# Seven quarter products per group in the first multiplication, the nonlinearity split, and one sum by transfer

## The chip, the cores and the metric

One core of one Trainium2 chip runs the whole computation in one launch. The metric is the device time of the program in microseconds (us), and lower is better. The core's engines work side by side, each through a queue of its own in program order: TensorE (PE, with its weight loads as PEld), VectorE (DVE), ScalarE (ACT), GpSimd (POOL), and SyncE (SP), which issues transfers.

## The reference

Attention with a causal window of 64, for 8 batches, 8 heads, 576 positions and 64 channels, is followed by a feed-forward layer with a PReLU between its two products. All arrays are fp32.

```python
scores = (q @ k.T) / sqrt(64);  mask = (0 <= rel) & (rel < 64)
attn = softmax(where(mask, scores, -1e9));  a = attn @ v
x = a.transpose(0, 2, 1, 3).reshape(4608, 512)
h = x @ w_in                              # 512 x 2048
g = maximum(h, 0) + alpha * minimum(h, 0) # alpha: one value for each of the 2048 columns
out = g @ w_out                           # 2048 x 512
```

The kernel returns `out`, 4608 x 512.

## The kernel before

The 4608 tokens are 36 tiles of 128, and four tiles make a block (9 blocks, `BT` = 4). Every fp32 product is made of three products of split numbers: a value is the sum of a high part (`xh`, `wh`) and a low part (`xl`, `wl`), and hi*hi, hi*lo and lo*hi are accumulated.

**First stage.** For each block, 16 cells (`cell`, L621), one for each 128 of the 2048 columns of `w_in`: 12 matmuls of 512 tokens (3 splits by 4 slices of the 512 channels, L637) into one of two PSUM banks. ACT reads the bank and writes slope*h to an SBUF cell (L643), DVE makes the PReLU from the bank and the cell (L644), and SP stores the cell to DRAM (`hidden`, L648). Attention runs between the cells. Twice in a block there is a turn (`attend_two`, L592): scores of two tiles (L444), then the values of the two tiles before (L500). Between the two, DVE takes the row minimum (L453), ACT the exponential (L460), POOL scales (L469), and the weights are turned by 16 small DVE transposes for each tile (L477, L479), or for the tiles in `PE_TURNED` and the first eight by PE (L484) with a copy out of PSUM (L488). `x_parts` (L561) splits the result into the block's x.

`w_in` and `w_out` come as raw 64-bit words and are converted on the chip (`chunk`, L332). `convert_out` (L376) forms the seven combinations of `w_out`'s quarters that the second stage needs, for one of four groups d (`DUOS`) at a time, in blocks 1, 3, 5 and 7. Slots 0 to 11 of `w_hi` and `w_lo` keep twelve of the 28 forms; the other 16 go to DRAM in two parts, and come back into `w_in`'s slots 12 to 27 at the end of the first stage (`fetch_weights`, L666).

**Second stage.** For each block and d (36 units, `second`, L691), the four quarters of g (a11, a12, a21, a22) are fetched (L701, issued up to 45 us of planned time ahead). DVE makes four sums z1 to z4 (L708). Seven forms are split into y parts by ACT (L713) and DVE (L714), and seven products of 12 matmuls with 256 columns (L741) accumulate over d in seven PSUM banks. These are the seven products of Strassen's scheme in Winograd's form, in place of eight. After four units, ACT (L758) and DVE (L749) add the banks up to the block of `out`.

**Order.** Each operation is registered with `Program.add`, with its durations, reads and writes. `Program.order` (L84) simulates the engines and writes out every engine's queue in that order: on each engine the ready operation with the earliest due time goes next. PE's due times are the keys (`begin_of`, `CELL`, `UNIT`, `STEP`); those of the others follow from what waits for them. While no real product is ready at the start, PE gets dummy matmuls (`warm`, L304), until the first cell.

## Time and profile before

| | |
|---|---|
| median of 3 runs | 844.79 us (844.37 to 847.77) |
| the profiled execution | 848.35 us |
| its span, first to last instruction | 846.6 us |
| PE busy | 838.7 us (99%) |
| DVE busy | 690.4 us (82%) |
| ACT busy | 446.5 us (53%) |
| POOL busy | 201.0 us (24%) |

The span is 1.75 us shorter than the execution's own time, and that execution took 3.56 us more than the median. Busy time is the union of an engine's instructions. PE's instructions overlap in the pipeline, so the distance between two starts says what one costs, and its duration does not. The profile's rows that are used are in a section of their own below.

### The profile page before, as it was taken

How to read it: one execution, taken by the hardware profiler on the slowest of the kernel's cores; microseconds unless marked ns; L12 is line 12 of the kernel's file. 1: busy time of each engine (PE TensorE's matmuls, PEld its weight loads, DVE VectorE, ACT ScalarE, POOL GpSimd, SP SyncE). 2: the span in 40 equal slices, each digit the busy share in tenths (PEclk: the TensorE clock that was granted, in tenths of full speed). 3: DMA queues.
4: the chain of work that ended last, by engine and by line, in shares of the span. 5: the costliest groups of instructions: out<-in, count | busy, mean ns of one | idle time of the engine just before them, and what ended most of it. 6: DMA issues, size and time to landing. Idle time of an engine off the chain costs nothing.

```text
span 846.6 us, 21125 instructions
## 1 busy us (share of the span) xinstructions
PE 838.7 (99%) x7856; PEld 760.3 (90%) x7856; DVE 690.4 (82%) x1775; ACT 446.5 (53%) x1130; POOL 201.0 (24%) x188
## 2 busy tenths in 40 slices
PE   9899999999999999999999999999999999999998
PEld 8788888888888888888888889999999999999998
DVE  5777898997989989899884547979888888979883
ACT  6789765556554664546644334444444444444441
POOL 5788492106511164212640000000000000000000
PEclk9899999999999999999999999999999999999999
DMA  7787755555655667556556997535444443535211
GB/s 235 235 275 240 232 173 165 168 177 190 205 174 163 209 219 252 192 176 216 196 204 184 316 330 231 165 110 168 121 148 138 136 151 125 154 110 169 83 37 50
DMA packets 121287, 152.91 MB, mean 181 GB/s; under 512 B 10592, under 2 KB 92512, under 8 KB 121184
## 3 DMA queue, kind: packets, MB, share of 16 engines
q1 hardware_dynamic: 120896, 151.30, 55.7%
q8 instruction: 62, 1.02, 0.5%
q14 instruction: 41, 0.34, 0.1%
q10 hardware_dynamic: 288, 0.26, 0.1%
HBM read 95.95 MB, written 55.57 MB: 179 GB/s over the span
## 4 chain that ended last, share of the span: by engine, by line
PE 97%; ACT 2%; DVE 1%; issue 0%; POOL 0%; POOLq 0%; DVEq 0%
PE bank L637 47%; PE bank L741 41%; PE bank L500 4%; PE bank L444 4%; ACT w L460 1%; PE bank L484 1%; PE bank L304 0%; DVE xl L570 0%; DVE val L366 0%; DVE bank L364 0%; ACT val L356 0%; DVE alphas L310 0%; ACT pt L488 0%; DVE cell L749 0%; DVE bank L353 0%
## 5 line engine op out<-in xcount | busy, mean ns | idle before, releaser
L713 ACT CAST yh<-g 128x512 fp32r<-128x512 f32 x216 | 133.4, 623 | 138.0 <-PE bank L741 96.1
L643 ACT ACTIVATE cell<-bank,alphas 128x512 f32<-128x512 f32 (+1 forms) x147 | 99.6, 678 | 166.7 <-PE bank L637 159.7
L714 DVE TENSOR_TENSOR yl<-g,yh 128x512 fp32r<-128x512 f32 x216 | 148.1, 689 | 27.9 <-ACT yh L713 26.6
L637 PE MATMUL bank<-xh,wh 128*128 128x512 f32 (+1 forms) x588 | 158.6, 392 | 0.0
L741 PE MATMUL bank<-wh,yh 128*128 128x256 f32 x1008 | 155.4, 276 | 0.0
L741 PE MATMUL bank<-wh,yl 128*128 128x256 f32 x1008 | 155.4, 276 | 0.0
L741 PE MATMUL bank<-wl,yh 128*128 128x256 f32 x1008 | 155.4, 276 | 0.0
L637 PE MATMUL bank<-xl,wh 128*128 128x512 f32 (+1 forms) x588 | 155.3, 386 | 0.0
L637 PE MATMUL bank<-xh,wl 128*128 128x512 f32 (+1 forms) x588 | 155.0, 385 | 0.0
L644 DVE SCALAR_TENSOR_TENSOR cell<-bank,alphas,cell 128x512 f32<-128x512 f32 (+1 forms) x147 | 108.5, 739 | 54.7 <-ACT cell L643 47.8
L741 PEld LDWEIGHTS bank<-wh,yh 128*128 128x128 f32 x1008 | 133.2, 188 | 0.1
L741 PEld LDWEIGHTS bank<-wl,yh 128*128 128x128 f32 x1008 | 133.1, 188 | 0.0
L741 PEld LDWEIGHTS bank<-wh,yl 128*128 128x128 f32 x1008 | 133.1, 188 | 0.0
L637 PEld LDWEIGHTS bank<-xl,wh 128*128 128x128 f32 x588 | 109.6, 189 | 22.5
L637 PEld LDWEIGHTS bank<-xh,wl 128*128 128x128 f32 x588 | 109.6, 189 | 22.1
L637 PEld LDWEIGHTS bank<-xh,wh 128*128 128x128 f32 x588 | 107.6, 189 | 23.0 <-DVE cell L644 0.9
L460 ACT ACTIVATE w<-w,nm 128x128 f32<-128x128 f32 x288 | 111.6, 390 | 23.5 <-DVE nm L453 23.5
L469 POOL TENSOR_TENSOR w<-w,rc 128x512 f32<-128x512 f32 x72 | 74.3, 1053 | 134.8 <-DVE rc L465 114.9
L477 DVE STREAM_TRANSPOSE pt<-w 32x256 f32<-32x256 f32 x192 | 83.7, 436 | 9.5 <-POOL w L469 6.2
L708 DVE TENSOR_TENSOR g<-g,g 128x512 f32<-128x512 f32 x108 | 74.4, 689 | 1.8
L453 DVE CUSTOM_DVE_ANT_0 w<-bank,masks 128x128 f32<-128x128 f32 x288 | 62.9, 285 | 9.5 <-PE bank L444 9.5
L479 DVE STREAM_TRANSPOSE pt<-w 32x128 f32<-32x128 f32 x192 | 58.1, 303 | 3.9
(64 smaller groups left out, 708.1 us busy)
## 6 DMA issues: line engine op xcount, KB each, us to landing
g<-g SPq DMA_DIRECT2D x144, 256.0 KB, 3.3
g<-cell SPq DMA_DIRECT2D x141, 256.0 KB, 3.1
out<-cell SPq DMA_DIRECT2D x36, 256.0 KB, 2.6
q<-qT SPq DMA_DIRECT2D x35, 256.0 KB, 5.0
raw<-w_out SPq DMA_DIRECT2D x16, 512.0 KB, 4.8
v<-vN SPq DMA_DIRECT2D x18, 384.0 KB, 5.4
k<-kT SPq DMA_DIRECT2D x17, 384.0 KB, 4.4
raw<-w_in SPq DMA_DIRECT2D x11, 512.0 KB, 5.5
```

Of the source, the lines that this page charges most:

```text
L453: nc.vector.tensor_tensor_reduce(out=of_head(weights[t % 2], g), in0=bank_of(S_BANK[t % 2][x])[:, e].rearrange("p (b k) -> p b k", b=2), i ...
L460: nc.scalar.activation(w, w, AF.Exp, scale=-1.0, bias=least[t % 2][:, g:g + 1], accum_out=sums[:, t % 2, g, 0:1])
L469: nc.gpsimd.tensor_tensor(out=w, in0=w, in1=rc.unsqueeze(1).unsqueeze(3).broadcast_to(list(w.shape)), op=ALU.mult)
L477: nc.vector.transpose(to, w[:, x, j])
L479: nc.vector.transpose(to[:, :, j ^ 1], w[:, x, j, :, j ^ 1])
L637: nc.tensor.matmul(h, w[KEPT + f][:, a * P:(a + 1) * P], v[:, a, half], start=k == a == 0, stop=k == 2 and a == NP - 1, skip_group_check=True)
L643: add(f"sl.{name}", "ACT", 0.13 + 0.46 * part, lambda: nc.scalar.activation(g, h, AF.Copy, scale=slope[:, f:f + 1]), ["signs", *k_h], k_g)
L644: add(f"la.{name}", "DVE", 0.12 + 0.61 * part, lambda: nc.vector.scalar_tensor_tensor(out=g, in0=h, scalar=sign[:, f:f + 1], in1=g, op0=AL ...
L708: add(name, "DVE", 0.61, lambda: nc.vector.tensor_tensor(out=to(), in0=a(), in1=b(), op=op), reads, writes)
L713: add(f"ys.{u}.{i}.h", "ACT", 0.54, lambda: nc.scalar.copy(y_of(y_hi, x, hi), value()), [*ks, "late"], his)
L714: add(f"ys.{u}.{i}.l", "DVE", 0.61, lambda: nc.vector.tensor_tensor(out=y_of(y_lo, x, lo), in0=value(), in1=y_of(y_hi, x, hi).bitcast(F32) ...
L741: nc.tensor.matmul(banks[bank][:, h * EH:(h + 1) * EH], part[:, j * HW + h * P:j * HW + (h + 1) * P], w[k][:, j * EH:(j + 1) * EH], start= ...
```

## The change

**Products.** In blocks 2 to 8 (`N0` = 2) `group(n, d)` replaces four cells. The x of a block and `w_in` are taken by quarters, as in the second stage, so seven products of 12 matmuls with 256 columns stand in place of 48 matmuls with 512. Four banks are used: X and Z (banks 4 and 5, from attention) and Y and V (the former two cell banks, swapped at every group). Sums between products are made in PSUM. The weight forms are made from `w_in`'s parts in block 0 (`forms_in`, into slots 0 to 11) and after block 1's cells (`last_form_in`); the four forms of each block's x in `forms_x`.

```diff
+    def group(n, d, base):
+        X, Z = S_BANK[1]
+        Y, V = H_BANK if grouped[0] % 2 == 0 else H_BANK[::-1]
...
+        def product(at, i, bank, new):      # 2 halves j x 3 splits x 2 slices of 256 columns
...
+            add(f"p.{n}.{d}.{i}", "PE", STEP, emit, ..., key=base + (at * STEP if at < 5 else VISIT * STEP - HOLD))
+        def out(bank, m, x):
...
+            late = 2 * m + x in LATE.get(n, ())
+            for j in range(2):
+                if late:
+                    add("sl...", "ACT", 0.36, ... activation(g, h, AF.Copy, scale=sign[:, f:f + 1]))
+                    continue
+                add("sl...", "ACT", 0.36, ... activation(g, h, AF.Copy, scale=slope[:, f:f + 1]))
+                add("la...", "DVE", 0.43, ... scalar_tensor_tensor(out=g, in0=h, scalar=sign[:, f:f + 1], in1=g, op0=ALU.mult, op1=ALU.max))
+            add("gs...", "SP", 0.5, ... dma_start(hidden[n][d][:, 2 * m + x], cells[c]), service=0.9)
...
+        product(0, 1, X, True)
+        add(f"pu.{n}.{d}", "ACT", 0.5, lambda: nc.scalar.copy(sums_of[0], banks[X]), kX, ["r.0"])
+        product(1, 6, Y, True)
+        sum_in("pb", banks[Y], kY, banks[Y], sums_of[0], ["r.0"])
+        product(2, 5, Z, True)
+        add(f"pz.{n}.{d}", "ACT", 0.5, lambda: nc.scalar.copy(sums_of[0], banks[Z]), kZ, ["r.0"])
+        sum_in("pc", banks[V], kV, banks[Y], sums_of[0], [*kY, "r.0"])
+        product(3, 2, X, False)
+        out(X, 0, 0)
+        product(4, 7, Y, False)
+        sum_in("pd", banks[Z], kZ, banks[Y], sums_of[0], [*kY, "r.0"])
+        out(Z, 1, 1)
+        product(5, 3, V, False)
+        out(V, 0, 1)
+        product(6, 4, Y, False)
+        out(Y, 1, 0)
```

`forms_x(n)` makes its four forms with six sums (DVE or POOL, 128x512) and four splits (a copy on ACT or POOL, a difference on DVE or POOL). In `quarter_parts` two of a block's quarters of x are kept as sums in `stage`.

**Nonlinearity.** For the quarters in `LATE`, only ACT reads the bank (sign*h), and DVE finishes when g has come back; these are 2, 4, 3, 1, 3, 2 and 0 of the 4 quarters in blocks 2 to 8, each for all four d.

```diff
+LATE = {2: (0, 1), 3: (0, 1, 2, 3), 4: (0, 2, 3), 5: (2,), 6: (0, 2, 3), 7: (0, 1), 8: (), 1: ()}
+                for j in range(2 if (q if n >= N0 else q % 2) in LATE.get(n, ()) else 0):
+                    def bend(s=s, q=q, j=j, f=f):
+                        nc.vector.scalar_tensor_tensor(out=g, in0=g, scalar=alpha_p[:, f:f + 1], in1=g, op0=ALU.mult, op1=ALU.max)
+                    add(f"lb.{u}.{q}.{j}", "DVE", 0.36, bend, (), [f"g.{s}.{q}"], paired=True)
```

**One sum by transfer.** From unit 2 on, z1 is an accumulating transfer from POOL's queue.

```diff
+BY_DMA = 2
+            def joined(name, to, a, reads, writes):
+                add(name, "POOL", 0.9, lambda: nc.gpsimd.dma_start(to(), a(), accum_op=ALU.add), reads, writes, service=1.6)
+            if u >= BY_DMA:
+                joined(f"z1.{u}", a21, a22, k22, k21)
```

**Attention.** A turn is cut in two: the first tile's scores come four cells (`pace`) ahead, the second's at the turn, both into banks 2 and 3. PE turns the weights of eleven tiles instead of four.

```diff
-PE_TURNED = (9, 17, 25, 33)
+PE_TURNED = (8, 14, 17, 18, 22, 25, 27, 28, 30, 31, 35)
+            score_of(ts[0], begin - pace, ())
+            softmax(ts[0])
+            score_of(ts[1], begin, [k for t in before for k in pt_keys(t)])
```

**`w_out`.** Its forms go to DRAM unsplit, all 28, in blocks 4 to 7 (`CONVERT_AT`). They come back into slots that the last block's groups leave free, and are split then (28 copies on ACT or POOL, 28 differences on DVE or POOL).

```diff
-CONVERT_AT = {1: 0, 3: 1, 5: 2, 7: 3}
+CONVERT_AT = {4: 0, 5: 1, 6: 2, 7: 3}
+        add(f"wf.{k}", "SP", 0.5, lambda: nc.sync.dma_start(value, scratch[k]), [f"far.{k}"], los, service=0.9)
+        split(f"ws.{k}", value, los, w_hi[slot], w_lo[slot], his, los)
```

**Memory.** What the second stage needs is opened in two parts: `right` (the y parts and g set 0) when attention and conversion are done, `left` (g sets 1 to 3) when the last block's x forms have been read.

**Start and planner.** Due times and the planner's constants are new. A gap in PE's planned order of over 0.4 us up to 48 us is filled with dummy matmuls in a spare bank (`without_lulls`). `alpha` comes by ACT's queue.

```diff
-BEGIN = 11.0
+BEGIN = 24.0
-SINGLE = (3.0, 3.0, 11.0, 13.0, 23.0, 32.0, 37.0, 41.0)
-HALVES = (12.0, 19.0)
+SINGLE = (0.5, 0.5, 6.5, 12.5, 29.0, 31.0, 35.0, 37.5)
+HALVES = (15.0, 19.0)
-PACE = 3.6
-FIRST_TURN = 60.0
+PACE = 3.4000000000000004
+FIRST_TURN = 54.0
+N0 = 2
+CELL2 = 3.1500000000000004
```

## Rows read from the trace of the kernel before

**Rows 1.** Page, part 4: the chain that ended last, by engine.

```profile
PE 97%; ACT 2%; DVE 1%; issue 0%; POOL 0%; POOLq 0%; DVEq 0%
```

**Rows 2.** Busy time by stretch: stretch, its us, engines busy (instructions), clock, DMA, GB/s.

```profile
0.00:23.20 23.20, 21.24 (x299) 19.46 (x300) 13.24 (x56) 14.16 (x47) 13.26 (x22) 1.00 0.82 247
23.20:40.00 16.80, 14.73 (x218) 13.08 (x217) 12.26 (x53) 13.93 (x49) 12.11 (x11) 0.80 0.69 219
...
145.00:455.40 310.40, 310.40 (x3038) 260.95 (x3037) 272.24 (x882) 166.54 (x507) 104.84 (x93) 1.00 0.58 191
455.40:499.40 44.00, 43.96 (x193) 35.74 (x192) 22.57 (x34) 16.74 (x26) 0.00 (x0) 1.00 0.92 298
499.40:846.60 347.20, 343.38 (x3025) 343.15 (x3023) 282.20 (x442) 154.26 (x252) 0.00 (x0) 1.00 0.44 138
```

**Rows 3.** The chain in order of time: start us, us, engine, line, instructions.

```profile
212.93 21.98 PE bank L637 x96
...
238.63 21.99 PE bank L637 x96
...
499.60 343.20 PE bank L741 x3024
```

**Rows 4.** PE's timeline, one turn: start, us, line, operation, shapes, count.

```profile
208.19 1.04 PE L484 MATMUL bank<-ident,w 128*128 128x128 f32 x8
209.15 1.98 PE L444 MATMUL bank<-k,q 64*64 64x128 f32 x64
210.95 1.98 PE L500 MATMUL bank<-pt,v 64*64 64x128 f32 x96
212.86 1.20 PE L637 MATMUL bank<-xh,wh 128*128 128x512 f32 x4
213.90 1.07 PE L637 MATMUL bank<-xl,wh 128*128 128x512 f32 x4
```

**Rows 5.** PE's timeline: matmuls of 256 columns, early block 0 and second stage.

```profile
43.96 0.64 PE L637 MATMUL bank<-xh,wh 128*128 128x256 f32 x4
...
44.91 0.64 PE L637 MATMUL bank<-xh,wl 128*128 128x256 f32 x4
...
499.90 0.63 PE L741 MATMUL bank<-wl,yh 128*128 128x256 f32 x4
...
509.84 0.63 PE L741 MATMUL bank<-wl,yh 128*128 128x256 f32 x4
```

**Rows 6.** Timeline: a cell's last products, the next cell, and the drain of its bank.

```profile
477.68 1.07 PE L637 MATMUL bank<-xh,wh 128*128 128x512 f32 x4
477.88 0.69 ACT L643 ACTIVATE cell<-bank,alphas 128x512 f32<-128x512 f32 x1 [2.03 <-PE bank L637]
...
478.60 0.75 DVE L644 SCALAR_TENSOR_TENSOR cell<-bank,alphas,cell 128x512 f32<-128x512 f32 x1 [1.97 <-ACT cell L643]
```

**Rows 7.** Timeline: the pair where a cell waited for DVE.

```profile
462.78 0.75 DVE L644 SCALAR_TENSOR_TENSOR cell<-bank,alphas,cell 128x512 f32<-128x512 f32 x1
...
463.58 0.76 PEld L637 LDWEIGHTS bank<-xh,wh 128*128 128x128 f32 x4 [0.43 <-DVE cell L644]
```

**Rows 8.** Groups by line and form: count, busy us, mean ns, idle before.

```profile
L477 DVE STREAM_TRANSPOSE pt<-w 32x256 f32<-32x256 f32 x192 | 83.7, 436 | 9.5 <-POOL w L469 6.2
...
L479 DVE STREAM_TRANSPOSE pt<-w 32x128 f32<-32x128 f32 x192 | 58.1, 303 | 3.9
...
L749 DVE TENSOR_TENSOR r<-bank,r 128x512 f32<-128x512 f32 x27 | 18.5, 684 | 1.9 <-PE bank L741 1.9
...
L644 DVE SCALAR_TENSOR_TENSOR cell<-bank,alphas,cell 128x256 f32<-128x256 f32 x6 | 2.8, 482 | 2.3 <-ACT cell L643 2.2
...
L758 ACT COPY r<-bank 128x512 f32<-128x512 f32 x9 | 5.3, 589 | 14.4 <-PE bank L741 14.4
...
L304 PE MATMUL bank<-ident 128*128 128x128 f32 x92 | 14.2, 310 | 1.4 <-POOL ident L288 1.4
```

**Rows 9.** Transfers: queue, count, KB each, median us to landing.

```profile
g<-g SPq DMA_DIRECT2D x144, 256.0 KB, 3.3
```

More of the change, by code (lines that the diff above doesn't have):

```diff
@@ L39 @@
 RAWS = 3
+N0 = 2
+CELL2 = 3.1500000000000004
+SIGNS = 8.3
 SHIFTED = {}
@@ L81, in add @@
             self.ops[a].then.append(o.at)
+        o.banks, o.fresh = ({int(b.split(".")[1]) for b in bs if b.startswith("bank.")} for bs in ((*reads, *writes), writes))
+        o.fresh -= {int(b.split(".")[1]) for b in reads if b.startswith("bank.")}
         self.ops.append(o)
@@ L156, in order @@
                     o.busy *= 1 + (now < warm_at)
-                if e == "POOL" and o.busy or e == "DVE" and o.paired:
+                if e == "PE":
+                    quarters, before = o.name[:2] == "p.", lately[0][:2] == "p."
+                    if quarters:
+                        steady = steady and before and now - lately[1] < 0.05
+                        entry = o.name[-1] == "7"
+                        o.busy = ENTRY if entry else STEP if steady else SLOW
+                        steady = steady or entry
+                    o.busy += CHANGE * (quarters != before)
+                    lately = o.name, now + o.busy
+                if e == "POOL" and o.busy and not o.service or e == "DVE" and o.paired:
                     o.busy += max(0.0, shared - now)
@@ L189, in order, with without_lulls, spare @@
             raise RuntimeError("the order stops short")
-        return order
+        return self.without_lulls(order, fill[1])
+    def without_lulls(self, order, first):
+        spans = [[] for _ in range(8)]
+        for at, o in order:
+            for b in o.banks if o else ():
+                spans[b].append((at, at + o.busy + LAGS[o.engine], b in o.fresh))
+        def spare(at):
+            for b in SPARE_ORDER:
+                here = [s for s in spans[b] if s[0] <= at]
+                later = [s for s in spans[b] if s[0] > at]
+                if here and max(s[1] for s in here) <= at - 0.2 and later and later[0][0] > at + FILL and later[0][2]:
+                    return b
+        dummies, idle_from, begun = [], None, False
+        for at, o in order:
+            if o is None or o.engine != "PE" or at > LULLS_UNTIL:
+                continue
+            if begun and at - idle_from > LULL:
+                while idle_from + FILL < at:
+                    b = spare(idle_from)
+                    if b is not None:
+                        dummies.append((idle_from, b))
+                    idle_from += FILL
+            begun, idle_from = begun or o.name == first, at + o.busy
+        placed = []
+        for at, o in order:
+            while dummies and dummies[0][0] <= at:
+                self.fillers[dummies[0][0]] = dummies[0][1]
+                placed.append((dummies.pop(0)[0], None))
+            placed.append((at, o))
+        return placed
 @with_exitstack
@@ L260, in banded_attention_then_prelu_ffn @@
     delta = work.tile([P, 512], F32, name="delta")
-    stage = work.tile([P, 2, 512], F32, name="stage")
-    staged = [stage[:, i] for i in range(2)]
+    work.tile([P, 24], F32, name="rim")
     raws.append(stage.rearrange("p x t -> p (x t)").bitcast(I32))
@@ L279, in banded_attention_then_prelu_ffn @@
     early_keys = set()
+    staged = [[f"staged.{i}.{x}" for x in range(2)] for i in range(2)]
     def keys(*names):
@@ L301, in guard_and_masks, with warm @@
             nc.gpsimd.memset(masks[h * W:(h + 1) * W, 1 + h, 0:W], NEG)
-    def warm():
-        nc.tensor.matmul(banks[H_BANK[1]][:, :P], ident, ident, start=True, stop=True)
-    add("alpha", "SP", 0.5, lambda: nc.sync.dma_start(alpha_p, alpha.rearrange("(f p) -> p f", p=P)), writes=["alpha"], service=0.6, earliest=3.0)
+    def warm(bank):
+        nc.tensor.matmul(banks[bank][:, :P], ident, ident, start=True, stop=True)
+    add("alpha", "ACT", 2.0, lambda: nc.scalar.dma_start(alpha_p, alpha.rearrange("(f p) -> p f", p=P)), writes=["alpha"], service=0.6, key=-900.0)
     def signs():
@@ new lines, in forms_x, with form @@
+    def forms_x(n):
+        t1, t2 = (stage[:, i].rearrange("p (x t) -> p x t", x=2) for i in range(2))
+        k1, k2 = staged
+        ((a11h, a11l), (k11h, k11l)), ((a12h, a12l), (k12h, k12l)) = (([v.bitcast(F32) for v in vs], ks) for vs, ks in (x_form(n, 1), x_form(n, 2)))
+        def form(i, value, k):
+            (hi, lo), (his, los) = x_form(n, i)
+            split(f"sx.{n}.{i}", value, k, hi, lo, his, los)
+        form(5, t1, k1)
+        two(f"s2a.{n}", t1, t1, a11h, ALU.subtract, k11h, k1)
+        two(f"s2b.{n}", t1, t1, a11l, ALU.subtract, k11l, k1)
+        form(6, t1, k1)
+        two(f"s3a.{n}", t2, a11h, t2, ALU.subtract, k11h, k2)
+        two(f"s3b.{n}", t2, t2, a11l, ALU.add, k11l, k2)
+        form(7, t2, k2)
+        two(f"s4a.{n}", t1, a12h, t1, ALU.subtract, k12h, k1)
+        two(f"s4b.{n}", t1, t1, a12l, ALU.add, k12l, k1)
+        form(3, t1, k1)
@@ L654, in banded_attention_then_prelu_ffn @@
     y_hi, y_lo, ring = [], [], {"at": 0}
-    SHIFTS = [(1, 1)] * 4 + [(i, i) for i in range(4)] + [(1, 1)] * 280
+    SHIFTS = [(2, 2) if x == 6 and turn in LEADS else (1, 1) for turn in range(26) for x in range(10)]
     def new_slot():
```

334 lines of the change are left out of this document (229 added, 105 removed).

## The prediction

> **What bounds the kernel now.** I read the chain that ended last first: 97% of it is PE [rows 1]. Busy time by stretch shows where [rows 2]: from block 2 on PE is busy in every microsecond, through 310.4 us of blocks 2 to 7, 44 us of block 8 and 343 us of the second stage, at the full clock. Only the first 40 us hold time in which PE had no product to do. The chain in order of time gives the pattern [rows 3]: eight cells take 21.98 us, the next eight begin 25.70 us after them, so a turn of attention takes 3.7 us, and a block 51.4 us. The second stage is 343.20 us without a break. So a saving on PE counts in full as long as the other engines keep up, and each new wait of PE counts in full too. DVE is next: 272.24 of 310.40 us (88%) in blocks 2 to 7, and 282.20 of 347.20 us (81%) in the second stage [rows 2].
>
> **Products.** Sixteen cells of a block take 2 x 21.98 = 43.96 us [rows 3]. The first four matmuls after a turn take 1.04 us (212.86 to 213.90) [rows 4], where four of an eight-cell run take 21.98 / 24 = 0.92 on average. That entry cost of 0.12, twice in a block, stays, so the products themselves are 43.7 us. The new ones are 28 products of 12 matmuls with 256 columns. The trace has two cadences for this shape [rows 5]: in block 0 eight of them take 0.95 us (119 ns each), and at the start of the second stage 84 take 9.94 us (118 ns); the whole second stage averages 343.20 / 3024 = 113.5 ns [rows 3], so the rest of it ran at about 113.3. A product is 1.42 or 1.36 us and a block's 28 are 39.7 or 38.1. Breaks for attention speak for the slow cadence, the long runs between them for the fast one; I take the middle, 38.9. That saves 4.8 us a block (4.0 to 5.6), over seven blocks **-33.6** (-28.0 to -39.2).
>
> A rule of the Trainium skill speaks against this step. "TensorE: Matmul & The Clock Gate", section "Back-to-back issue gap", has streams of weight load and matmul at about 131 ns for 512 columns and 81 ns for 128. By an estimate from it, 192 matmuls would be 25 us and 336 of 256 columns at least 27 us, and quarters would lose. The trace does not agree: 512 columns take 229 ns (21.98 / 96) [rows 3], twice the 113.5 of 256.
>
> **Attention on PE.** PE turns seven tiles more; one costs 209.15 - 208.19 = 0.96 us [rows 4]: **+6.7**. Cutting 14 turns in two adds an entry of at least 0.12 each, and a change out of the products; I take 0.25: **+3.5** (1.7 to 5.6). Scores now have one pair of banks. The second tile's scores wait until DVE has taken the first's row minima, which has four cells' time, over 10 us: nothing. Before any wait, PE has 33.6 - 6.7 - 3.5 = 23.4 us less to do.
>
> **New waits in a group.** A cell had the other bank to go on with. In a group the fifth product (7) goes into Y, which the sum pc must have read; pc waits for pz, ACT's copy of Z, and Z is complete when the third product ends. Rows 6 and 7 give the chain: ACT starts 0.20 after the next product has begun (477.68 to 477.88), a copy of a bank takes 0.59 [rows 8], DVE follows 0.03 later (478.60), its sum takes 0.68 [rows 8], and PE goes on 0.05 after DVE (462.78 + 0.75 to 463.58) [rows 7]: 1.56 us. One product (2), 1.36 to 1.42 us, covers it. The bare wait is 0.14 to 0.20 in each of 28 groups. The other chains have more cover: pd with 0.97 us has product 3 behind it, and a bank that the next group needs has two products. But ACT and DVE work in order, and whatever stands ahead of pz or pc on them is added, with all of PE's queue behind it. At 88% busy a pass of 0.68 us stands ahead often; half of one is 0.34. Rows 7 show this already: in block 8, where y work joins the cells, PE waits 0.43 us for DVE although a cell has over 2 us of slack. Against it, attention can fill some of the gaps. I take 0.4 us a group: **+11.2** (0.15 to 0.8: 4.2 to 22.4).
>
> **DVE in blocks 2 to 7.** It loses 16 transposes for each of seven tiles, (83.7 + 58.1) / 24 = 5.9 us a tile [rows 8], 41 us, and 96 PReLU passes of 0.75 [rows 6], 72 us. It gains 72 passes on half a bank (nine quarters of g that are not late, by four d, by two halves) of 0.48 [rows 8], 35 us, 24 x 3 sums of 0.68, 49 us, and up to 10 passes a block for the x forms, 0 to 41 us, since POOL is busy only 104.84 of 310.40 us [rows 2] and can take them. That is 243 to 292 us of about 300: 81 to 97%, no bound in itself, but near it. ACT was at 54% there and gains two copies and four short drains a group. The forms of `w_in`, made in blocks 0 and 1, are needed at block 2 only and cost nothing unless POOL and DVE are late there; their cover is about 50 us.
>
> **Start.** No product begins before 23 us, dummies fill 14.2 us [rows 8], and from 23.2 to 40 us the clock averages 0.80 [rows 2]: 6.7 us at 1.2 instead of 2.4 GHz, worth 3.4 us. Filled lulls can win that, third and fourth tiles due earlier can take a dummy's place, and the first cell due at 15 instead of 12 can lose it again. No row shows the new order; I take **-3.5** (-7 to +4).
>
> **Border.** Unit 0 is prepared during block 8. Unit 1's g comes after the last x form is read, one product before the end: 3.3 us to land [rows 9], then a copy and a difference of some 0.7 us each, about 5 us, under unit 0's 343.20 / 36 = 9.53 us. The 28 fetches and splits are needed seven by seven, 9.53 us apart, and POOL was idle there [rows 2]. **0** (0 to 4); without the cover, one landing.
>
> **Second stage.** A unit costs DVE 282.2 / 36 = 7.8 of 9.53 us. z1 goes in 34 units (-0.68 each), and 15 late quarters x 4 x 2 = 120 passes come, at 0.48: 282 - 23 + 58 = 317 us, 92%. In block 3, with all four quarters late, a unit needs 7.8 - 0.7 + 3.8 = 10.9 us, so DVE falls 4 x 1.4 = 5.6 us behind; in blocks 4 and 6 it is 2 us each. Passes on g can run up to three units ahead, and ten y slots leave three products (4 us) in hand. No row shows an accumulating transfer: the nearest is a fetch of g, 3.3 us [rows 9], or two of them, 6.6, as it also reads its destination. With g three units (29 us) ahead both are hidden; POOL has nothing else, and z2, z4 and four forms queue on DVE behind a late one. **+1** (0 to 10).
>
> **Sum.** -33.6 + 6.7 + 3.5 + 11.2 - 3.5 + 0 + 1 = -14.7 us. The profiled execution would go from 848.35 to 833.7; the median of runs, 3.56 us lower, from 844.79 to **830**.
>
> **The rivals.** (a) *The chain is covered.* Attention fills the gaps, the wait is the bare 0.2 us and the fast cadence holds: -39.2 + 6.7 + 3.5 + 5.6 - 3.5 = -26.9, **818**. For it: one gap per group, and attention pieces that can be put there. Against it: DVE at 88%. (b) *The second stage runs late.* Block 3's late passes, or late z1s, stop PE, which also puts products back on the 118 ns cadence, 0.06 us each [rows 5]: 5.6 us behind plus 50 to 100 slow products, some +9, **838**. For it: 10.9 against 9.53 us; against it, the lead in g. The Trainium skill has a rule for this case: "SBUF — State Buffer", section "SBUF: two separate sides" (the box on SWDGE), says that a DVE pass in a two-port mode keeps POOL from writing the descriptors of its transfers. No run here shows it, and by the page itself sums of two tensors are not in that mode. (c) *The group's waits eat the gain.* ACT and DVE queue ahead of pz, pc and pd in every group, and PE waits 1.2 us in each: 28 x 1.2 = 33.6, -23.4 + 33.6 - 3.5 + 1 = +7.7, **852**. The place is product 7 of each group; it decides from (23.4 + 3.5 - 1) / 28 = 0.93 us a group. For it: three in-order hand-overs in a chain that is longer than its cover; against it, rows 7, where a crowded DVE cost 0.43. (d) *It does not shorten the block.* The softmax chain from score to turned weights, not PE, sets the distance of turns, and blocks 2 to 7 stay at 51.4: then block 8 (-4.8) and the start are all, **837** to **845**. Against it: DVE has fewer transposes.
>
> **How the numbers follow.** The forecast has 0.50 (822 to 839), (a) 0.20, (b) 0.13, (c) 0.13, (d) 0.04. About 0.5% (4.2 us) is what a measurement can tell from no change, so faster means under 840.6 and slower over 849.0. Faster: nearly all of the forecast, (a), two thirds of (b): 0.77. Slower: (c) save its low end, 0.12. Same: the rest, 0.11. The range 815 to 844 leaves out the best of (a) and all of (c), under 0.2.
>
> **What would show it.** Right: blocks 2 to 7 about 49.9 us long; 256-column matmuls at 113 to 119 ns there; PE waits on DVE at the fifth product of a group, some 11 us in total; second stage 343 to 345 us. Wrong: PE idle over 0.9 us a group; waits on y in the second stage around its units 12 to 19 with matmuls back at 118 ns; a gap of more than 4 us between the stages; a later first cell than 23 us.

## The result, and the profile after

The changed kernel takes 834.08 us (median of 4 runs, 833.64 to 834.99); the kernel before, on the same chip, 845.09 (4 runs, 844.37 to 847.77). The ratio is 0.9865, 95% interval 0.9842 to 0.9889. The forecast was 830. The span of the profiled execution went from 846.6 to 832.1 us. Of 40 more executions of the kernel before, 25 span 842.2 to 844.7 us at a mean granted clock of 0.999 or 1.000, and 15 span 844.9 to 846.2 us at 0.996 or 0.997, where the profiled one (846.6 us, 0.996) belongs. First the page of after: busy time of each engine, and the chain that ended last by engine.

```profile
PE 820.7 (99%) x8950; PEld 791.3 (95%) x8950; DVE 693.1 (83%) x1835; ACT 507.7 (61%) x1379; POOL 404.5 (49%) x399
...
PE 71%; DVE 5%; ACT 2%; issue 1%; DMA 0%; SPq 0%; ACTq 0%; DVEq 0%
```

PE bounds the kernel still. The chain can be followed back to 168 us only, so its shares add up to 79% of the span. In that part it is 90% PE, where it was 97% [rows 1]: it leaves PE for DVE and ACT at times. POOL's work has doubled. Busy time by stretch of after, cut at the first product, at blocks 2 and 8 and at the last group's end (columns as in rows 2):

```profile
0.00:21.99 21.99, 19.87 (x295) 18.32 (x295) 11.16 (x56) 14.65 (x47) 12.03 (x22) 1.00 0.83 251
21.99:40.00 18.01, 18.01 (x272) 16.91 (x269) 15.53 (x67) 16.28 (x61) 16.31 (x16) 1.00 0.82 265
...
145.26:437.29 292.03, 290.75 (x3921) 283.27 (x3920) 240.06 (x815) 220.76 (x701) 196.89 (x186) 1.00 0.62 206
437.29:488.00 50.71, 46.66 (x374) 46.04 (x373) 29.95 (x53) 31.45 (x68) 39.26 (x31) 0.93 0.74 231
488.00:832.10 344.10, 340.15 (x2990) 339.96 (x2988) 307.90 (x539) 148.65 (x261) 38.81 (x41) 1.00 0.60 166
```

Together with before this accounts for the whole span. In before, the first matmul of block 2 starts at 145.90 us, that of block 8 at 455.25 and that of the second stage at 499.43; rows 2 are cut at 145.00, 455.40 and 499.40, so blocks 2 to 7 took 309.4 us there and not 310.4. Block 8 of after holds the first three products of the second stage, 4.25 us of its 50.7; they are counted with the second stage here. "Forecast" is the sum of the terms of the prediction that lie in that stretch: in blocks 2 to 7, for instance, six blocks of products (-28.8), the turned tiles (+6.7), twelve cut turns (+3.0) and 24 groups at 0.4 (+9.6).

| stretch | before, us | after, us | difference | forecast |
|---|---|---|---|---|
| up to block 2 | 145.9 | 145.3 | -0.6 | -3.0 |
| blocks 2 to 7 | 309.4 | 292.0 | -17.3 | -9.5 |
| block 8 | 44.2 | 46.5 | +2.3 | -3.2 |
| second stage | 347.2 | 348.4 | +1.2 | +1 |
| span | 846.6 | 832.1 | -14.5 | -14.7 |

(Each is rounded by itself.) So the total is that of the forecast in the trace, but blocks 2 to 7 won 7.8 us more than it says, and the start (2.4) and block 8 (5.5) gave those back.

**Where blocks 2 to 7 won.** Distances from each matmul's start to the next, summed by line, give: products 263.7 before and 239.2 after (39.3 us a block within the products, where 38.9 was forecast, and some 0.6 a block between them), weights turned 2.9 and 9.3, scores 19.8 and 20.8, values 23.0 and 22.8. That is -24.5 + 6.4 + 1.0 - 0.2 = -17.3. The forecast's products and turns are there. Its group waits are not. The waits of PE in blocks 2 to 7 of after (us in all, times, longest):

```profile
PE bank L828 <- DVE bank L854: 1.0, 4, 0.3
```

By distances they are some 2.5 us in 24 groups, at product 7 and at the last one, 4, which waits for the sum pd: 0.1 a group, not 0.4. The timeline of one group of after shows why. PE takes its products in the order 1, 5, 2, 6, 7, 3, 4. The line at 200.14 is the end of 6, whose bank is Y; L854 at 200.64 is the sum pb, L861 is ACT's copy pz, L854 at 202.39 is the sum pc, and 203.30 is the start of product 7, which has to wait for pc:

```profile
200.14 0.39 PE L828 MATMUL bank<-xl,wh 128*128 128x256 f32 x2
200.46 1.10 PE L550 MATMUL bank<-k,q 64*64 64x128 f32 x32
200.64 0.70 DVE L854 TENSOR_TENSOR bank<-bank,r 128x512 f32<-128x512 f32 x1 [0.96 <-PE bank L828]
...
201.39 1.98 PE L606 MATMUL bank<-pt,v 64*64 64x128 f32 x96
201.78 0.58 ACT L861 COPY r<-bank 128x512 f32<-128x512 f32 x1
202.39 0.70 DVE L854 TENSOR_TENSOR bank<-bank,r 128x512 f32<-128x512 f32 x1
203.30 0.51 PE L828 MATMUL bank<-sh,wh 128*128 128x256 f32 x2
```

Z was complete long before (product 5 ended at 196.8). But pz overwrites the operand that pb reads, so it has to wait for pb, and pb for product 6. From the end of 6 to the end of pc this chain took 2.6 us. Scores and values, 2.84 us of PE, stand in the gap, and 7 starts 0.21 us after pc. In 23 of the 24 groups of blocks 2 to 7 attention stands between Z's last matmul and product 7, 1.0 to 3.6 us of it, beside product 2. In 18 groups pc is done 0.6 to 3.7 us before product 7 starts, in six 0.05 to 0.22 us before. The one group without attention, block 7's last, is one of the six: its product 7 starts 0.26 us late.

In most groups 6 goes ahead of 5, and the chain begins at Z as the prediction has it: 1.4 to 2.6 us from the end of 5 to the end of pc. In five groups here, and in two of block 8's, 5 goes ahead of 6, and pb is a further hand-over in the chain, which the prediction did not count.

**Where block 8 lost.** It has no attention. Its second group, in after:

```profile
450.52 0.68 DVE L956 TENSOR_TENSOR diff<-g,g 128x512 f32<-128x512 f32 x1
...
451.12 1.10 DVE L962 TENSOR_TENSOR yl<-g,yh 128x512 fp32r<-128x512 f32 x1
...
452.67 2.97 POOL L392 TENSOR_TENSOR wl<-wl,wh 128x512 fp32r<-128x512 f32 x2
...
452.94 1.57 DVE L956 TENSOR_TENSOR g<-g,g 128x512 f32<-128x512 f32 x1
...
454.43 0.69 DVE L854 TENSOR_TENSOR bank<-bank,r 128x512 f32<-128x512 f32 x1
...
455.03 1.15 DVE L956 TENSOR_TENSOR g<-g,g 128x512 f32<-128x512 f32 x1
455.21 0.59 ACT L861 COPY r<-bank 128x512 f32<-128x512 f32 x1
...
456.11 0.68 DVE L962 TENSOR_TENSOR yl<-g,yh 128x512 fp32r<-128x512 f32 x1
...
456.71 0.69 DVE L854 TENSOR_TENSOR bank<-bank,r 128x512 f32<-128x512 f32 x1
...
457.45 0.79 PE L828 MATMUL bank<-sh,wh 128*128 128x256 f32 x2 [3.20 <-DVE bank L854]
```

L956 and L962 are unit 0's sums and splits. The sum pb (454.43) stands behind one of them, pz (455.21) has to wait for pb, whose operand it overwrites, and pc (456.71) stands behind two more. Two of the three took 1.57 and 1.15 us, where L956 takes 0.68 at 450.52: POOL's passes at 452.67 run beside them. PE stands 3.2 us, and after it the clock is at half (busy time by stretch of after):

```profile
457.45:463.54 6.09, 6.09 (x29) 6.09 (x30) 2.61 (x5) 1.71 (x5) 4.70 (x3) 0.51 0.42 137
463.54:470.00 6.46, 6.46 (x59) 6.46 (x58) 4.81 (x10) 6.03 (x13) 3.68 (x3) 1.00 0.71 215
```

At 0.51 (the level of 1.2 GHz) the products that start at 457.45, 460.18 and 462.74 take 2.73, 2.56 and 1.72 us from start to start instead of 1.36, some 2.9 us lost. With this group's wait of 3.4 us by distance, and two of 0.5 and 0.6 in the first group, that is 7.4 us; the other 39.0 of block 8's 46.5 us are its products, as forecast.

**The second stage** has no gap of PE after its start in after, although DVE is busy 307.90 of 344.10 us there, against 282.20 of 347.20 [rows 2]. The added passes and the transfer that takes a sum from DVE are these lines of after, with the landing time of the transfers (accumulating ones on POOLq):

```profile
L945 DVE SCALAR_TENSOR_TENSOR g<-g,alphas 128x256 f32<-128x256 f32 x120 | 53.8, 479 | 0.0
...
L953 POOL DMA_DIRECT2D g<-g x34 | 29.8, 875 | 275.2 <-DVE yl L962 141.0 <-ACT yh L961 45.4 <-DVE r L1000 27.9
...
g<-g SPq DMA_DIRECT2D x144, 256.0 KB, 4.5
g<-g POOLq DMA_DIRECT2D x34, 256.0 KB, 4.6
```

120 passes at 479 ns are what the prediction counted from rows 8. A fetch of g lands in 4.5 us instead of 3.3 [rows 9], and an accumulating transfer, for which no row stood, in 4.6.

### The profile page after: what moved, and what is told of

It reads as the page before. It is cut to its first block, busy times and chain, and to the rows that moved or that the text cites. A ratio compares the mean times of both kernels' runs of the same rounds, so it can differ in the third digit from the quotient of the medians.

```text
span 832.1 us, 23734 instructions
## 1 busy us (share of the span) xinstructions
PE 820.7 (99%) x8950; PEld 791.3 (95%) x8950; DVE 693.1 (83%) x1835; ACT 507.7 (61%) x1379; POOL 404.5 (49%) x399
## 3 DMA queue, kind: packets, MB, share of 16 engines
q8 instruction: 70, 1.15, 0.6%
## 4 chain that ended last, share of the span: by engine, by line
PE 71%; DVE 5%; ACT 2%; issue 1%; DMA 0%; SPq 0%; ACTq 0%; DVEq 0%
PE bank L992 41%; PE bank L828 25%; PE bank L550 2%; PE bank L606 2%; DVE pt L583 1%; DVE bank L854 1%; DVE pt L585 1%; ACT w L566 1%; PE bank L590 1%; DVE cell L848 1%; DVE w L559 1%; DMA g<-g 0%; ACT cell L847 0%; DVE g L956 0%; ACT cell L843 0%
## 5 line engine op out<-in xcount | busy, mean ns | idle before, releaser
L953 POOL DMA_DIRECT2D g<-g x34 | 29.8, 875 | 275.2 <-DVE yl L962 141.0
L962 DVE TENSOR_TENSOR yl<-g,yh 128x512 fp32r<-128x512 f32 x216 | 147.0, 706 | 2.9 <-ACT yh L961 2.6
L828 PE MATMUL bank<-xh,wh 128*128 128x256 f32 x560 | 113.4, 284 | 1.4 <-DVE bank L854 0.8
L828 PE MATMUL bank<-xh,wl 128*128 128x256 f32 x560 | 110.3, 279 | 0.0
L828 PE MATMUL bank<-xl,wh 128*128 128x256 f32 x560 | 110.0, 278 | 0.0
L828 PEld LDWEIGHTS bank<-xh,wh 128*128 128x128 f32 x560 | 85.3, 189 | 5.1 <-DVE bank L854 1.6
L828 PEld LDWEIGHTS bank<-xh,wl 128*128 128x128 f32 x560 | 85.5, 190 | 0.0
L828 PEld LDWEIGHTS bank<-xl,wh 128*128 128x128 f32 x560 | 85.2, 189 | 0.0
L854 DVE TENSOR_TENSOR bank<-bank,r 128x512 f32<-128x512 f32 x84 | 58.4, 696 | 27.3 <-PE bank L828 15.3
L956 DVE TENSOR_TENSOR g<-g,g 128x512 f32<-128x512 f32 x74 | 52.2, 705 | 18.8 <-DMA g<-g 18.4
L848 DVE SCALAR_TENSOR_TENSOR cell<-bank,alphas,cell 128x256 f32<-128x256 f32 x104 | 45.2, 479 | 26.8 <-ACT cell L847 26.3
L443 POOL TENSOR_TENSOR val<-val,ulps 128x512 int32<-128x512 int32 x32 | 42.3, 1327 | 46.8 <-DVE val L435 40.9
```

The source lines that it names most:

```text
L443: add("jn." + name, "POOL", 1.27, lambda: nc.gpsimd.tensor_tensor(out=bits, in0=bits, in1=ulps, op=ALU.add), [k_ulps], [k_val, *both], ear ...
L828: nc.tensor.matmul(h, at_place(w, place)[:, c * P:(c + 1) * P], v[:, c], start=new and j == 0 and not done, stop=j == 1 and done == 5, ski ...
L848: add(f"la.{n}.{d}.{m}.{x}.{j}", "DVE", 0.43, lambda h=h, g=g, f=f: nc.vector.scalar_tensor_tensor(out=g, in0=h, scalar=sign[:, f:f + 1], ...
L854: add(f"{name}.{n}.{d}", "DVE", 0.6, lambda: nc.vector.tensor_tensor(out=to, in0=a, in1=b, op=ALU.add), reads, k_to)
L953: add(name, "POOL", 0.9, lambda: nc.gpsimd.dma_start(to(), a(), accum_op=ALU.add), reads, writes, service=1.6)
L956: add(name, "DVE", 0.61, lambda: nc.vector.tensor_tensor(out=to(), in0=a(), in1=b(), op=op), reads, writes, paired=True)
```

## The experiments

Ratios are against executions of the kernel before that ran beside each experiment. Three questions: what the waits in a group depend on, whether the second stage lives on the transfer, and what the late passes and the weights turned on PE are worth.

**1. The sum pc made twice as long.** Every group issues pc two times, in the same order of all queues.

```diff
+            def emit():
+                for _ in range(2 if name == "pc" else 1):
+                    nc.vector.tensor_tensor(out=to, in0=a, in1=b, op=ALU.add)
```

> The sum pc is issued twice in each of the 28 groups (the second writes the same values), and the written order is left as it is. DVE has 0.6 us more in each group, between Z's copy and product 7. Theory A, a piece of attention stands between Z's last matmul and product 7 in nearly every group of blocks 2 to 7 and covers the chain: blocks 2 to 7 grow by at most 0.2 us a group, 5 us in all, and only block 8, which has no attention, waits the full 0.6 in some groups; 834 goes to 835 to 841. Theory B, the chain from Z to product 7 sets the pace of the groups: every group grows by 0.6 us, 28 x 0.6 = 17 us, to 851.

Measured: 843.92 us, ratio 0.9985 (0.9965 to 1.0004). Blocks 2 to 7 take 302.8 us, 10.8 more, or 0.45 a group; the second stage is as it was. PE's waits in blocks 2 to 7 of this kernel (the sum is at L856 here):

```profile
PE bank L828 <- DVE bank L856: 8.0, 17, 1.5
```

0.45 lies between the two theories. Attention does cover the chain, but 0.7 us more on DVE, in a stretch where others queue too, uses the cover up in part of the groups: PE's waits go from 4 to 17, and product 7 waits in 8 of the 24 groups. In block 8 theory A's longer waits came (1.3 us at product 7 of the first group, where after has 0.5), but no half clock behind them, and the block is 2 us shorter than in after. The whole takes nearly all of the change's gain away.

**2. Quarters from the fifth block on only.**

```diff
-N0 = 2
+N0 = 4
```

> Quarters from block 4 on instead of block 2 on; blocks 2 and 3 are cells again, all else as changed (the forms of w_in are made two blocks later, too). Theory A, the gain lies in PE's products of blocks 2 to 7 and is the same for each block, 18.4 us over six: 3.1 us less attention's new pieces, which stay, so blocks 2 and 3 grow by 43.7 - 39.3 = 4.4 us each at most: 834 goes to about 842. Theory B, what blocks 2 and 3 give is taken back elsewhere (making the forms on DVE and POOL in blocks 0 and 1): less than 4 us, to under 838.

Measured: 872.47 us, ratio 1.0341 (1.0301 to 1.0382). Neither theory. The first stage is longer by some 9 us, as it should be with two blocks of cells. But the second stage takes 375.5 us where that of after takes 348.4 (here and below its products in block 8 are counted in), with some 24 us of gaps of PE by start-to-start distance that after does not have, and DVE waits there for accumulating transfers (waits of DVE in this kernel, then in after):

```profile
DVE g L956 <- DMA g<-g: 42.6, 23, 4.9
```

```profile
DVE g L956 <- DMA g<-g: 18.4, 12, 3.3
```

The edit does a little more than its name: in a block of cells `LATE` counts by halves of the columns, so all four quarters of block 2 are late, and the second stage has 136 late passes instead of 120. So the run tells nothing clean of the quarters; the ninth experiment repeats it without the transfer. It turned the question to the transfer.

**3. Unit 0 not prepared in block 8.** Its four fetches of g are held back by 42 us of planned time, so that none of its passes can stand ahead of pc.

```diff
-                    ["left" if s else "right", *(f"far.g.{n}.{d}.{q}.{j}" for j in range(2))], [f"g.{s}.{q}"], service=0.9, earliest=base - 45)
+                    ["left" if s else "right", *(f"far.g.{n}.{d}.{q}.{j}" for j in range(2))], [f"g.{s}.{q}"], service=0.9, earliest=base - (45 if u else 3))
```

> Unit 0's four g transfers are issued 42 us of planned time later, after block 8's groups, so no sum or split of unit 0 runs on DVE and ACT during block 8, and no product of the second stage stands between its groups. The stages are then apart by the preparation of unit 0, some 10 to 20 us. Theory A, PE's waits and half-clock time in block 8 come from unit 0's sums on DVE ahead of pc: products and waits of block 8 alone go from 46.4 to about 40 to 41 us, with bare waits of 0.15 to 0.6 a group and no drop of the clock. Theory B, they come from the groups' own chain without attention to fill it: each of the four groups waits 0.5 to 1 us or more, and block 8 stays at 43 us or above.

Measured: 872.33 us (one run). Block 8 takes 41.8 us, at full clock. Its third and fourth groups wait 0.21 us each at product 7, with nothing of attention beside them: the bare chain that the prediction put at 0.14 to 0.20. In the timeline of this kernel, third group, the start of product 7 comes 0.44 us after the matmuls before it, where 0.23 is the rhythm:

```profile
467.76 0.39 PE L828 MATMUL bank<-xh,wl 128*128 128x256 f32 x2
467.99 0.39 PE L828 MATMUL bank<-xl,wh 128*128 128x256 f32 x2
468.43 0.50 PE L828 MATMUL bank<-sh,wh 128*128 128x256 f32 x2
468.77 0.39 PE L828 MATMUL bank<-sh,wl 128*128 128x256 f32 x2
```

So unit 0's passes, with the half clock behind their wait, are what made block 8 of after 4.7 us longer. Waits of 0.69 and 0.54 in the first group and of 0.95 in the second stay, and so are not theirs: in the second group 5 goes ahead of 6, and the chain with pb has one product (2) as cover. Of the 3.4 us that this group waits in after, some 2.4 are unit 0's. The price is elsewhere: PE stands 12.1 us ahead of the second stage, which takes 375.8 us, with 22 us of gaps at the starts of its blocks from unit 12 on, and with 50.9 us of DVE's waits on DMA. The second stage of this kernel begins with nothing in hand and never gets ahead; whether that is the transfer's doing, the next three tell.

**4, 5 and 6. No late passes; z1 on DVE; both.**

```diff
-LATE = {2: (0, 1), 3: (0, 1, 2, 3), 4: (0, 2, 3), 5: (2,), 6: (0, 2, 3), 7: (0, 1), 8: (), 1: ()}
+LATE = {}
```

```diff
-BY_DMA = 2
+BY_DMA = 99
```

> No quarter is late: DVE makes the whole PReLU in the first stage (120 half passes of 0.48 us more there, 58 us) and none in the second stage. Theory A, DVE is near its limit in blocks 2 to 7 and the late passes keep it under: blocks 2 to 7 grow by 10 us or more, with PE waiting on DVE's cells and sums, and the second stage stays at 344. Theory B, DVE has room in both stages: within 4 us of 834.

> All 36 sums z1 are made by DVE again and none by an accumulating transfer; all else as changed. DVE gets 34 x 0.6 = 20 us more in the second stage, 308 + 20 = 328 of 344 us (95%). Theory A, the transfer buys DVE time that the late passes need: without it PE waits in the second stage from about unit 12 (the block with all quarters late) on, some 3 to 15 us, 837 to 849. Theory B, DVE has room, and the transfer only adds a latency of about 5 us in the chain of each unit: the second stage stays at 344 us and the time at 834.

> No late quarters, and z1 by DVE in every unit: the run without late quarters (882.6) again, with the transfer taken out of the second stage. There PE had gaps at the start of each block from unit 12 on while DVE stood idle for 87 us in waits on an accumulating transfer. Theory A, the transfer is what makes the y parts late once the second stage starts without work in hand: the gaps at the block starts go, the second stage takes 344 to 348 us instead of 368, 882.6 goes to about 860. Theory B, the gaps come from the late start of the second stage itself (the sums of a block ahead of y work on DVE): they stay, and so does the time, 875 or more.

Measured: 882.57 (no late passes, one run), 834.00, ratio 0.9854 (0.9834 to 0.9875) (z1 on DVE), 870.79 (both, one run). Without the transfer the time is that of the change: it buys nothing here. DVE carries z1 with no room left, and PE still has no gap (busy time by stretch, z1 on DVE):

```profile
591.00:701.00 110.00, 110.00 (x973) 110.00 (x972) 109.95 (x204) 49.36 (x84) 0.00 (x0) 1.00 0.45 142
701.00:801.00 100.00, 100.00 (x884) 100.00 (x884) 99.90 (x179) 44.79 (x77) 0.00 (x0) 1.00 0.41 128
```

Without late passes DVE has 120 passes less in the second stage (53.8 us in after), and with the transfer the stage is nevertheless full of gaps (13.5 us at block starts; DVE waits 87.0 us for the transfers, 26 times) and takes 372.6 us; with z1 on DVE they are gone but for unit 0, and it takes 353.2. So the gaps belong to the transfer: z2 reads what z1 makes and stands behind it on DVE in program order, and z1's landing of about 5 us is idle time there unless it was issued early enough.

The late passes themselves: without them blocks 2 to 7 take 302.5 us, 10.5 more than after, with DVE at 276.39 us of these instead of 240.06. That is what they are worth there, with all that follows from them in the order of the queues.

Both kernels also begin the second stage late, PE waiting 13 us. It is the conversion of `w_out` on POOL: its last pass ends at 432.9 us in after, at 496.3 without late passes, at 503.9 with both edits, and the first product of the second stage comes 12 us after it in the last two (508.2 and 515.9). How that goes is shown with the twelfth.

**7 and 8. Unit 0 out of pc's way, gently.** One fetches unit 0's g 11 us of planned time later; the other tells only the planner that unit 0's passes on DVE take 1.0 us.

```diff
-                    ["left" if s else "right", *(f"far.g.{n}.{d}.{q}.{j}" for j in range(2))], [f"g.{s}.{q}"], service=0.9, earliest=base - 45)
+                    ["left" if s else "right", *(f"far.g.{n}.{d}.{q}.{j}" for j in range(2))], [f"g.{s}.{q}"], service=0.9, earliest=base - (45 if u else 34))
```

```diff
-                add(name, "DVE", 0.61, lambda: nc.vector.tensor_tensor(out=to(), in0=a(), in1=b(), op=op), reads, writes, paired=True)
+                add(name, "DVE", 1.0 if name.endswith(".0") else 0.61, lambda: nc.vector.tensor_tensor(out=to(), in0=a(), in1=b(), op=op), reads, writes, paired=True)
...
-                add(f"ys.{u}.{i}.l", "DVE", 0.61, lambda: nc.vector.tensor_tensor(out=y_of(y_lo, x, lo), in0=value(), in1=y_of(y_hi, x, hi).bitcast(F32), op=ALU.subtract),
+                add(f"ys.{u}.{i}.l", "DVE", 1.0 if u == 0 else 0.61, lambda: nc.vector.tensor_tensor(out=y_of(y_lo, x, lo), in0=value(), in1=y_of(y_hi, x, hi).bitcast(F32), op=ALU.subtract),
```

> Unit 0's g is fetched 11 us of planned time later (34 us ahead of its due time instead of 45), all else as changed. Its sums and splits then fall into block 8's third and fourth groups instead of the second. Theory A, the long wait in block 8 (3.4 us, and the half clock behind it) comes from these passes ahead of one pc: it goes, block 8 takes 42 to 44 us instead of 46.4, and if the second stage keeps its 344 us the time is 830 to 832. Theory B, what the second stage has in hand at its start counts for more: block 8 is shorter, but gaps at the starts of blocks in the second stage take it back, 834 to 850.

> In the planner alone, DVE's passes of unit 0 last 1.0 us instead of 0.61, as those of the trace did that ran beside POOL (1.10, 1.57 and 1.15 us); nothing is computed otherwise. Theory A, the order that the short duration gave put three of these passes ahead of a group's sum pc: with the longer one the planner leaves the gap alone, PE's wait of 3.4 us goes, 829 to 832. Theory B, the order is of no matter, POOL's passes beside them are: the wait stays between 2 and 4 us, 833 to 838.

Measured: 832.38 us, ratio 0.9846 (0.9819 to 0.9874), and 841.22, ratio 0.9935 (0.9912 to 0.9958). With the later fetch no wait in block 8 is above 1.0 us and the clock is full through it:

```profile
437.40:483.00 45.60, 42.93 (x364) 41.92 (x364) 31.32 (x55) 30.37 (x65) 32.35 (x26) 1.00 0.80 259
```

With the planner's edit the long wait falls to 1.8 us and the clock holds too, but from unit 20 on the second stage has gaps at the starts of blocks, 7.0 us in all, and nearly every unit from 25 on runs at 118 ns a matmul instead of 113; neither theory foresaw that. DVE waits 31.5 us for transfers there (18.4 in after).

**9. Quarters from the fifth block, with z1 on DVE.** The second and the fifth edit together.

> Quarters from block 4 on, and z1 by DVE in every unit: the run with quarters from block 4 on (872.5) without the transfer in the second stage, where PE had 23 us of gaps. Theory A, those gaps came from the transfer once the second stage had little work in hand, and a block of quarters is worth about 3 us: the second stage takes 344 to 350 us, and the time is 834 + 2 x 3 = 840 to 847. Theory B, blocks 2 and 3 are needed as quarters for what the second stage has in hand: the gaps stay, 860 or more.

Measured: 854.31 us, ratio 1.0109 (1.0081 to 1.0136). Blocks 2 and 3 as cells take 107.3 us and as quarters 98.2 (48.8 + 49.4): 4.6 us a block. The time lies between the two theories. The 4.6 is the gain of the quarters in a block where attention fills the gap, with the same tiles turned on PE. The second stage takes 356.0 us where the second experiment's takes 375.5, so most of the gaps there came from the transfer. Some 5 us of gaps in units 0 and 1 remain, and 3 us in units 13 to 17, whose cause the runs do not tell, so the stage is 7.6 us longer than that of after, and the kernel ends above the one before.

**10 and 11. The seventh and the eighth with z1 on DVE.**

> Unit 0's g 11 us later in the plan (832.4 alone) and z1 by DVE in every unit (834.0 alone). Theory A, both the pc that is held up in block 8 and the latency of the transfer are gone, and DVE has room for z1: 830 to 833, no gap in the second stage after unit 1. Theory B, DVE at 95% without the transfer has no room for the later start: gaps from unit 12 on, 835 or more.

> Unit 0's passes planned at 1.0 us (841.2 alone, with 12 us of gaps in the second stage from unit 20 on) and z1 by DVE in every unit. Theory A, the gaps came from the transfer's latency and not from too much work on DVE: they go, the wait in block 8 stays short (1.9 us, no half clock), 828 to 832. Theory B, they came from DVE's work: they stay or grow, 840 or more.

Measured: 831.81 us, ratio 0.9847 (0.9821 to 0.9873), and 832.78, ratio 0.9840 (0.9818 to 0.9862). Neither has a gap of over 0.2 us in the second stage after unit 1. The eleventh differs from the eighth only in the transfer, and its second stage takes 348.8 us instead of 360.4: the 841 of the eighth was the transfer's latency. With the seventh (832.38) these are the fastest of all, 1.3 to 2.3 us under the change by their medians, with intervals that overlap that of the change, so no gain over it is shown.

**12. Four tiles turned on PE, as before, with z1 on DVE.**

```diff
-PE_TURNED = (8, 14, 17, 18, 22, 25, 27, 28, 30, 31, 35)
+PE_TURNED = (9, 17, 25, 33)
```

> The kernel after with the four tiles that PE turned in the kernel before (9, 17, 25, 33) in place of eleven, and z1 on DVE in every unit, which by itself left the time at 834.0. PE has seven turns of 0.96 us less, 6.7 us, all of it in blocks 2 to 8; DVE has 16 transposes for each of seven tiles more, (59.2 + 41.2) / 17 = 5.9 us a tile, 41 us. Theory A, as the prediction costs it: turning is bare time on PE and DVE keeps up, at 240 + 41 = 281 of 285 us: blocks 2 to 7 take 286 instead of 292 us and the time is 827 to 828. Theory B: at 98% DVE is the bound, pc and pd queue behind transposes in every group, PE's waits at the fifth and last product of a group grow from about 2 us in these blocks to 15 or more, and the time is 838 to 850: the turns on PE are the price of the short group waits, and not a cost of their own.

Measured: 874.02 us, ratio 1.035 (1.0312 to 1.0388). Theory B, and more than it said. Blocks 2 to 7 take 312.3 us, longer than before the change:

```profile
144.93:457.20 312.27, 294.91 (x3865) 283.49 (x3864) 280.60 (x929) 210.30 (x683) 175.38 (x163) 0.98 0.54 176
```

DVE's 280.60 us are what was expected (281). PE has less to do, but the groups wait, and now attention itself waits for DVE (PE's waits in these blocks):

```profile
PE bank L550 <- DVE nm L559: 5.5, 4, 1.5
PE bank L828 <- ACT cell L843: 5.2, 6, 1.0
PE bank L828 <- DVE bank L854: 4.2, 6, 1.7
PE bank L606 <- DVE pt L585: 2.0, 2, 1.6
```

Of the rest of the loss, 13.5 us lie between the last group's end (505.9) and the first product of the second stage (519.4). Its chain in order of time (start us, us, engine, line) names the cause:

```profile
506.19 1.28 POOL val L392
507.47 0.02 issue
507.48 0.52 SPq L504
508.00 0.05 issue
508.05 4.61 DMA wl<-wo
512.66 0.02 issue
512.68 0.27 ACT wh L395
512.95 5.74 DMA g<-g
...
519.41 3.30 DVE yl L962
522.71 0.04 issue
522.75 7.26 PE bank L992 x49
```

POOL's last pass of the conversion, whose inputs come by way of DVE, ends at 507.5 instead of 432.9; then a weight form and g are fetched, 10 us of landings in a row (the memory for unit 0's g opens only when the conversion has ended), and the first product comes 12 us after that pass, as in the two kernels without late passes.

## Why the prediction was right, and where it was not

The forecast was right in sign and, in the trace, in size: -14.5 where the sum was -14.7. It was so because terms that were off cancelled, and that part was luck.

- **Products.** Right: 39.3 us a block against 38.9, in the two cadences of rows 5. By an estimate from the rule weighed there, of the Trainium skill ("TensorE: Matmul & The Clock Gate", section "Back-to-back issue gap"), they would have been at least 27 us against 25 for the cells, a loss. The trace does not agree: the products of a block take 39.9 us with what lies between them, where the cells took 43.9, so the trace's rows were the ones to go by. The ninth experiment gives 4.6 us a block for the whole step.
- **PE turns more tiles.** The price was right, 6.4 against 6.7 us. What it buys was counted (41 us of DVE) but not weighed: the prediction put DVE at 81 to 97% and called it no bound in itself, but near it. At 82% (240 of 292 us) it is none; at 90% (280 of 312, the twelfth) blocks 2 to 7 lose all that they had won, and the conversion of `w_out` runs so late that PE stands 13 us ahead of the second stage. The seven tiles are worth some 20 us in blocks 2 to 7 alone. The late passes are of the same kind, 10.5 us. DVE's share by itself does not tell the loss: without the late passes it is 91% (276 of 302.5), with half the loss.
- **Waits in a group.** The term that was mis-sized: 0.4 us in each of 28 groups was taken, and in blocks 2 to 7 they are 0.1. The bare chain was right where 6 goes ahead of 5 (0.21 measured in the third experiment against 0.14 to 0.20); where 5 goes ahead, pb lengthens it (0.95 in the same run). The step that failed is the 0.34 us, half of a pass on DVE that stands ahead, put into every group with attention named but not counted: the text had "one gap per group, and attention pieces that can be put there" as a rival's argument. In 23 of 24 groups attention is in the gap. Rival (a) is therefore right about the waits in blocks 2 to 7; about the cadence it is not, since 39.3 us a block lies between the slow 39.7 and the fast 38.1.
- **Block 8.** It has no pieces, and the forecast's -3.2 became +2.3. Rival (c)'s mechanism (passes queued ahead of pc) costs much here only, by unit 0's passes, which took up to 2.3 times as long beside POOL's. That the border costs 0 to 4 was within what the prediction allowed, but it put the cost on a fetch that lands late; none did.
- **Start.** -3.0 forecast with the cut turns of block 1, -0.6 measured. The filled lulls did win the clock back (0.80 [rows 2], now 1.00), and the first product comes 1.3 us earlier. But the dummies take 17.4 us by start-to-start distance instead of 13.7, 4.2 of them behind the first product. Block 1, with its cut turns, is 0.1 us longer. Of what is left the runs say nothing; no start was tried by itself. (What the clock's return is worth to the median is the last point of this list.)
- **Second stage.** Right in size, +1.2 against +1, and in the price of the late passes. What was not weighed is how near it is to failing. Rival (b) is what happened in four of the twelve kernels (the second, third, fourth and eighth), by late transfers; in after it did not. What keeps it off in after is not shown: the third and fourth kernels begin the stage with no product done in block 8, where after has three, but the eighth begins with four and has the gaps, and the seventh with two and has none after unit 1. DVE at 100% for 210 us (the fifth) did no harm.
- **From profile to median.** The medians differ by 11.0 us and the spans by 14.5. The prediction took off 3.56 us, because the profiled execution of before was that much above its median, and 3.5 us for the start, where half clock costs 3.4 us. By the granted clocks these are the same microseconds, counted twice. In the profile of before the granted clock is 0.5 from 31 to 38 us and full in all the rest but the last microsecond, which gives its mean of 0.996; most executions of before have a mean of 0.999 or 1.000, so they hold no such stretch, and the median is among them. The change can't win back there what was not lost. Without the -3.5 the sum is -11.2 and the forecast 833.6, against 834.08 measured. That the executions at 0.996 lose it at the same place is argued from the mean alone; one of them has a profile.

Not shown: which part of the loss at the start is due to which edit, and whether a plan with attention pieces left over for block 8 would win its 5 us; and what margin the transfer needs in the second stage.

## What to carry to other kernels

When a chain of hand-overs is a little longer than the work that covers it, look first at what else the bounding engine has to do that does not depend on it, and count its pieces against the gaps: attention in 23 of 24 gaps made 0.1 us of what was feared to be 0.4 to 1.2. Extra work on the bounding engine can be the price of that: seven turns cost PE 6.4 us, and without them the same blocks took 20 us longer, so an edit that looks like a loss on the critical engine has to be judged by what its neighbour would do without it. A transfer in place of a pass takes busy time off an engine but puts a landing of 5 us into an in-order queue: between kernels whose edits differ in nothing else it cost nothing (the change and the fifth) or 12 to 20 us of the second stage (the second and ninth, fourth and sixth, eighth and eleventh). And before a microsecond of the profile is counted as won, look whether the median execution has it to lose.

## What the runs showed of the hardware

**DVE beside POOL.** A sum or difference of two SBUF operands on DVE, 128x512, takes 0.68 us with POOL idle (450.52 and 456.11 in the timeline of block 8) and 1.10 to 1.57 us where it comes while POOL is at a pass (451.12, 452.94, 455.03). A sum of the groups, with one operand in PSUM, keeps its 0.69 beside POOL (454.43). Over the whole trace of after, 61 sums of the groups that overlap a pass of POOL take 0.70 us on average, as the other 23 do. The Trainium skill ("SBUF — State Buffer", section "Who interferes with whom") says that a DVE instruction with two SBUF inputs contends with a GpSimd instruction that reads SBUF, and that one with at most one SBUF input, outside the two-port modes, does not; the trace agrees (0.68 to 1.57 us for the one, 0.70 for the other).

**The clock after a wait.** A wait of 3.2 us was followed by 6.09 us at a granted clock of 0.51 in after; in the twelfth kernel one of 3.66 us by half clock too (0.66 from 480 to 485 us). In the first experiment's kernel a wait of 3.48 us at the same place was followed by none: 1.00 from 470 us on. A wait of this length can cost as much again, but need not.

**An accumulating transfer** of 256 KB from SBUF to SBUF occupies POOL's queue for 0.875 us and lands in 4.6 us (5.2 in the fourth kernel), about what a plain fetch of g takes in the same kernel (4.5).

**Two cadences.** Matmuls of 256 columns ran at 113 ns or at 118 ns for units on end, at the full granted clock. After a gap of PE in the second stage the slower one was seen to stay for units (the eighth kernel, to the end); what decides it was not found.
